# An attention and gated-convolution kernel rewritten: block-diagonal k^T v, one q*kv product, an on-chip spread of the norm factor, and an order written out as a list

## The chip, the core and the metric

The kernel runs on one core of one Trainium2 chip. The metric is device microseconds of one execution. The core's engines run side by side: TensorE (PE, with PEld for its weight loads), VectorE (DVE), ScalarE (ACT), GpSimd (POOL) and SyncE (SP); each takes its own instructions in order, and they wait for each other through semaphores. POOL and SP issue the DMAs. A figure such as 128x576 means partitions by elements.

## The reference

q, k and v are 8 batches x 8 heads x 576 positions x 64, in fp32.

```
kv  = einsum('bhsd,bhse->bhde', k, v)           # 64x64 for each head
out = einsum('bhsd,bhde->bhse', q, kv)
rms = sqrt(mean(out * out, axis=-1) + 1e-06)    # one factor per position and head
x   = out / rms * g_norm                        # heads side by side: (8, 576, 512)
h   = maximum(x @ w_in, 0)                      # w_in 512 x 1024
c   = conv_w[0]*h[s-1] + conv_w[1]*h[s] + conv_w[2]*h[s+1]   # along positions, zero at the ends
result = (h * sigmoid(c)) @ w_out               # w_out 1024 x 512, fp32
```

## The kernel before, in words

Matrices are bf16 in SBUF. Features lie on partitions: two heads fill 128 partitions, so 512 features are four tiles t, and the 1024 features of h are eight tiles f. A position s is 6p + r, p on 96 partitions, r along the row; the kernel keeps positions in a permuted order (by r first) up to the result.

The eight batches go in five groups, (0), (1, 2), (3, 4), (5, 6), (7). A group passes through these steps; the names in brackets are lines of the profile.

- load (L140): POOL issues casting DMAs for k, v and q of a batch, two buffers each; batch 0 comes in two halves. w_in comes in four pieces on SP's queue (L156), DVE scales and casts it (L157), and w_out comes on POOL's queue (L165).
- attn_a: k^T v by 48 matmuls of 96x64 per batch (L191), and four ACT copies of kv (L200); q is transposed by PE (L211) and copied by DVE (L214). out_mm (L267) makes q*kv for one tile with four matmuls of 64x64 and 288 columns. ACT squares it (L222), and a product with the small matrix sel sums the squares over each head's 64 partitions (L231).
- norm_unit: ACT takes Ln and Exp of the sums (L246, L247), SP stores the factor to DRAM (L249) and reads it back eight times, each row broadcast to 64 partitions (L254, tile rb).
- attn_b: out_mm makes q*kv a second time, and DVE multiplies it by rb into xT (L279).
- mm1: w_in's product (L300) in pieces of 384 or 288 columns, relu by ACT (L303). For every two f, DVE makes three tap products (L311) and six shifted adds (L315, L316; the permuted order cuts each shift into three), ACT the sigmoid (L317), DVE the gate product (L319).
- mm2: w_out's product, 8 matmuls of 512 columns for 128 positions (L336), copied out by ACT or, one time in three, DVE (L343, L341), and stored by SP in pieces (L350).

PSUM has separate pools: two slots for w_in's product, two for w_out's, one each for q*kv, the sums, and k^T v with the transposes. The order comes from interleave(): in stage s it mixes mm1 of group s, mm2 of group s - 1 and the attention of group s + 1, by weights written beside each unit. The framework may still move an instruction past others of its engine: in the trace a sigmoid stands between the Ln and the Exp of group 1, and each of these three has a table load of its own.

Of the kernel before, what the change touches and what calls it, by code (L numbers as in the profile page):

```python
# [56 lines left out]
DRAM = bass.MemoryType.DRAM  # L57

GROUPS = ((0,), (1, 2), (3, 4), (5, 6), (7,))


def interleave(*lists):

    keyed = []
    for n, units in enumerate(lists):
        total = float(sum(w for w, _ in units)) or 1.0
        at = 0.0
        for m, (w, fn) in enumerate(units):
            keyed.append(((at + 0.5 * w) / total, n, m, fn))
            at += w  # L70
    for _, _, _, fn in sorted(keyed, key=lambda x: x[:3]):
        fn()
# [3 lines left out]
def kernel(  # L76
# [39 lines left out]
    from concourse.masks import make_identity
    ident = consts.tile([P, P], BF16, name="ident")
    make_identity(nc, ident)
    ident32 = consts.tile([3 * n_ff, 3 * n_ff], FP32, name="ident32")
    make_identity(nc, ident32)  # L120
    eps_sb = consts.tile([P, 1], FP32, name="eps_sb")
    nc.vector.memset(eps_sb, eps)

    sel = consts.tile([P, 4, SM], BF16, name="sel")
    nc.vector.memset(sel, 0.0)
    for c in range(4):
        nc.vector.memset(sel[:D, c, 2 * c:2 * c + 1], 1.0)
        nc.vector.memset(sel[D:, c, 2 * c + 1:2 * c + 2], 1.0)

    qkv = {}

    def load(b, parts=1):
        hs = H // parts
        for i in range(parts):
            for name, src in (("k", k), ("v", v), ("q", q)):
                if i == 0:
                    qkv[name, b] = loads.tile([PS, H, R * D], BF16, name=name + "_sb")
                nc.gpsimd.dma_start(  # L140
                    out=qkv[name, b][:, i * hs:(i + 1) * hs, :],
                    in_=src[b, i * hs:(i + 1) * hs].rearrange("h (p r) d -> p h (r d)", r=R),
                )

    load(0, parts=2)

    w_in_sb = consts.tile([P, n_hd, D_ff], BF16, name="w_in_sb")
# [3 lines left out]
    cw_rows = consts.tile([3 * n_ff, P], FP32, name="cw_rows")  # L151
    nc.sync.dma_start(out=cw_rows, in_=moe_conv_w.rearrange("k (f p) -> (k f) p", p=P))
    w_stage = []
    for t in range(n_hd):
        st = loads.tile([P, D_ff], FP32, name="w_stage")
        nc.sync.dma_start(out=st, in_=moe_w_in[t * P:(t + 1) * P, :])  # L156
        nc.vector.tensor_scalar_mul(w_in_sb[:, t, :], st, g_sb[:, 0:1])  # L157
    cw_ps = ps_ss.tile([P, 3 * n_ff], FP32, name="cw_ps", tag="ss")
    nc.tensor.transpose(cw_ps, cw_rows, ident32)
    cw = consts.tile([P, 3 * n_ff], FP32, name="cw")  # L160
    nc.vector.tensor_copy(cw, cw_ps)

    load(1)
    w_out_sb = consts.tile([P, n_ff, D_model], BF16, name="w_out_sb")
    nc.gpsimd.dma_start(out=w_out_sb, in_=moe_w_out.rearrange("(f p) m -> p f m", p=P))  # L165
    load(2)


    class Group:
# [234 lines left out]
```

## Time and profile before

| | |
|---|---|
| runs, device us | 268.79, 271.13, 271.8 (median 271.13) |
| profiled execution, span | 268.2 us (the trace has no other time of it) |
| mean granted TensorE clock | 0.946 of full speed |
| PE busy, instructions | 200.9 us (75%), 1609 |
| DVE busy, instructions | 162.9 us (61%), 351 |
| ACT busy, instructions | 146.1 us (54%), 238 |
| DMA bytes written | 37.18 MB |

The span runs from the first to the last instruction. Busy time is the union of an engine's instructions. A busy PE is not at its peak: matmuls are pipelined, and a short group of them is charged its full latency. The profiler names what ended an engine's wait; of several it names the last.

### The profile page before, as it was taken

The numbers are of one execution on the slowest core, as the hardware profiler recorded it, in microseconds if no ns is written. First come the engines' busy times: TensorE is split into PE (matmuls) and PEld (weight loads), VectorE is DVE, ScalarE is ACT, GpSimd is POOL, SyncE is SP. The second block draws the span as 40 slices with busy tenths as digits, with TensorE's granted clock in tenths as the row PEclk, the third lists the DMA queues.
The fourth block names the chain that finished last, engine by engine and source line by source line (L and its number), as shares of the span: only waits on it lengthen the run. The fifth ranks groups of instructions, "written<-read, shape, count | busy, mean of one in ns | idle before, by whom it ended". The sixth has DMA issues, their size and how long they took to land.

```text
span 268.2 us, 4181 instructions
## 1 busy us (share of the span) xinstructions
PE 200.9 (75%) x1609; PEld 101.6 (38%) x1609; DVE 162.9 (61%) x351; ACT 146.1 (54%) x238; POOL 22.0 (8%) x36
## 2 busy tenths in 40 slices
PE   0118507989368879987289999883999899789953
PEld 0115303545133444433143444342344444444421
DVE  0222113678531577879884688858568879999521
ACT  1023302699922048998442789973249995665330
POOL 8321211011012121000000000000000000000000
PEclk9999999999867979999779999997799999999998
DMA  6999999995979999501954101396320254025423
GB/s 129 258 256 204 214 220 249 204 179 85 173 147 242 257 229 219 81 0 34 237 125 138 42 0 54 90 230 161 81 78 0 73 176 149 0 79 158 118 67 109
DMA packets 36006, 37.18 MB, mean 139 GB/s; under 512 B 2556, under 2 KB 30868, under 8 KB 35988
## 3 DMA queue, kind: packets, MB, share of 16 engines
q0 software_dynamic: 19904, 15.21, 37.2%
q1 hardware_dynamic: 16084, 21.73, 30.2%
q8 instruction: 12, 0.20, 0.3%
q14 instruction: 6, 0.05, 0.1%
HBM read 41.96 MB, written 10.17 MB: 194 GB/s over the span
## 4 chain that ended last, share of the span: by engine, by line
PE 42%; ACT 22%; DMA 14%; DVE 13%; issue 4%; SPq 3%; POOL 1%; DVEq 0%; POOLq 0%; ACTq 0%
PE h_ps L300 18%; PE o_ps L336 14%; ACT tap L317 8%; DMA rb<-scr 7%; DMA v_sb<-in_v_dram 5%; PE ot_ps L267 4%; ACT h L303 3%; DVE xT L279 3%; PE qT_ps L211 3%; SPq L254 3%; DVE tap L311 2%; PE ss_ps L231 2%; DVE h L319 2%; ACT L317 2%; ACT L247 2%
## 5 line engine op out<-in xcount | busy, mean ns | idle before, releaser
L336 PE MATMUL o_ps<-w_out_sb,h 128*128 128x512 bf16 (+1 forms) x296 | 78.3, 399 | 13.3 <-DVE h L319 12.0
L300 PE MATMUL h_ps<-xT,w_in_sb 128*128 128x384 bf16 (+1 forms) x416 | 82.7, 324 | 6.3 <-ACT h L303 5.8
L303 ACT ACTIVATE h<-h_ps 128x384 bf16<-128x384 f32 (+1 forms) x104 | 46.7, 464 | 25.4 <-PE h_ps L300 24.8
L311 DVE TENSOR_SCALAR tap<-h,cw 128x1152 bf16<-128x1152 bf16 (+1 forms) x120 | 47.8, 452 | 15.6 <-ACT h L303 15.4
L300 PEld LDWEIGHTS <-w_in_sb 128*128 128x128 bf16 x416 | 37.6, 99 | 37.0 <-issue 13.0
L336 PEld LDWEIGHTS <-h 128*128 128x128 bf16 (+1 forms) x296 | 28.3, 101 | 45.2 <-DVE h L319 14.8
L317 ACT ACTIVATE tap<-tap 128x2304 bf16<-128x2304 bf16 (+1 forms) x20 | 34.8, 1738 | 13.9 <-DVE tap L316 13.9
L279 DVE TENSOR_TENSOR xT<-ot_ps,rb 128x576 bf16<-128x576 f32 x32 | 24.1, 754 | 25.4 <-DMA rb<-scr 17.7
L200 ACT ACTIVATE kv_sb<-kv_ps 64x256 bf16<-64x256 f32 x32 | 12.1, 377 | 45.1 <-PE kv_ps L191 44.8
L267 PE MATMUL ot_ps<-qT,kv_sb 64*64 64x288 bf16 x256 | 23.0, 338 | 14.7 <-DVE xT L279 14.4
L319 DVE TENSOR_TENSOR h<-h,tap 128x2304 bf16<-128x2304 bf16 (+1 forms) x20 | 22.3, 1116 | 15.6 <-ACT tap L317 15.5
L343 ACT ACTIVATE o_sb<-o_ps 128x512 f32<-128x512 f32 (+1 forms) x25 | 14.9, 595 | 26.5 <-PE o_ps L336 24.5
L214 DVE COPY qT<-qT_ps 128x576 bf16<-128x576 bf16 x32 | 14.6, 455 | 22.5 <-PE qT_ps L211 22.3
L211 PE MATMUL qT_ps<-ident,q_sb 96*128 96x96 bf16 x192 | 18.6, 250 | 12.3 <-DVE qT L214 6.7
L316 DVE TENSOR_TENSOR tap<-tap,tap 128x1152 bf16<-128x1152 bf16 (+5 forms) x60 | 26.9, 471 | 0.0
L315 DVE TENSOR_TENSOR tap<-tap,tap 128x1152 bf16<-128x1152 bf16 (+5 forms) x60 | 26.8, 469 | 0.0
L222 ACT ACTIVATE sq<-ot_ps 128x576 bf16<-128x576 f32 x32 | 20.9, 652 | 5.5 <-PE ot_ps L267 5.4
L211 PEld LDWEIGHTS <-q_sb 96*128 96x128 bf16 x192 | 15.3, 123 | 19.7 <-issue 18.3
L267 PEld LDWEIGHTS <-kv_sb 64*64 64x64 bf16 x256 | 9.1, 108 | 32.7 <-issue 30.5
L191 PE MATMUL kv_ps<-v_sb,k_sb 96*64 96x64 bf16 x384 | 11.9, 218 | 10.5 <-DMA v_sb<-in_v_dram 10.5
L191 PEld LDWEIGHTS <-k_sb 96*64 96x64 bf16 x384 | 9.9, 131 | 15.0 <-issue 10.9
L341 DVE COPY o_sb<-o_ps 128x512 f32<-128x512 f32 x12 | 8.3, 689 | 6.8 <-PE o_ps L336 6.6
(26 smaller groups left out, 64.7 us busy)
## 6 DMA issues: line engine op xcount, KB each, us to landing
rb<-scr SPq DMA_DIRECT2D x24, 288.0 KB, 6.9
out_dram<-o_sb SPq DMA_DIRECT2D x24, 192.0 KB, 2.3
k_sb<-in_k_dram POOLq DMA_DIRECT2D x7, 576.0 KB, 12.1
v_sb<-in_v_dram POOLq DMA_DIRECT2D x7, 576.0 KB, 15.6
q_sb<-in_q_dram POOLq DMA_DIRECT2D x7, 576.0 KB, 12.7
out_dram<-o_sb SPq DMA_DIRECT2D x24, 128.0 KB, 2.3
rb<-scr SPq DMA_DIRECT2D x16, 144.0 KB, 4.9
w_stage<-in_moe_w_in_dram SPq DMA_DIRECT2D x4, 512.0 KB, 6.2
```

Of the source, the lines that this page charges most:

```text
L191: nc.tensor.matmul(ps[i * D:(i + 1) * D, hp, :], k_sb[:, 2 * hp + i, r * D:(r + 1) * D], v_sb[:, 2 * hp + i, r * D:(r + 1) * D], start=(r ...
L211: nc.tensor.transpose(ps[:, i, j * PS:(j + 1) * PS], q_sb[:, 2 * hp + i, j * P:(j + 1) * P], ident[:PS, :PS])
L267: nc.tensor.matmul(ps[i * D:(i + 1) * D, e, :HS], g.kv[bi][es, t, i, :], g.qT[bi][es, 2 * t + i, :], start=True, stop=True)
L279: nc.vector.tensor_mul(g.xT[:, t, bi * S:(bi + 1) * S].rearrange("p (e n) -> p e n", n=HS), ps[:, :, :HS], g.rb[:, t, 2 * bi:2 * bi + 2, :])
L300: nc.tensor.matmul(ps, w_in_sb[:, t, f * P:(f + 1) * P], g.xT[:, t, cs], start=(t == 0), stop=(t == n_hd - 1))
L303: nc.scalar.activation(g.h[:, f, cs], ps, AX.Relu)
L311: nc.vector.tensor_scalar_mul(taps[j][:, f, :], g.h[:, f0 + f, :], cw[:, col:col + 1])
L315: nc.vector.tensor_add(v[1][:, :, here], v[1][:, :, here], v[0][:, :, there])
L316: nc.vector.tensor_add(v[1][:, :, there], v[1][:, :, there], v[2][:, :, here])
L317: nc.scalar.activation(taps[1], taps[1], AX.Sigmoid)
L319: nc.vector.tensor_mul(hs, hs, taps[1])
L336: nc.tensor.matmul(ps[:n, :], g.h[:, f, t0:t0 + n], w_out_sb[:, f, :], start=(f == 0), stop=(f == n_ff - 1))
```

## The change

The kernel function is new almost throughout.

- The positions of xT, h and the result are in sequence order. The transposes of q keep the order by r (384 of 96x64 in place of 192 of 96x128); ACT's squares and copies of q*kv read PSUM with a step of 96 floats and write in sequence order. Batch 0 is squared without that step; its order changes in its multiply.
- kv of two heads is written into a 128x128 block-diagonal matrix (kvbd, zeros off the blocks), by two copies per batch (batch 0: one per tile and half). q*kv is one product of 576 columns per tile (ot), made once; ACT squares it (sq) and copies it to SBUF in fp32 (oc).
- Batch 0's norm: a product with ones (on) sums the squares and spreads the sum over the 64 partitions of its head at once; Ln and Exp (nl, nx) of 576 columns per tile, one multiply (mu0). The others go in groups (1), (2, 3), (4, 5), (6, 7): sums as before (ss), Ln, Exp (ln, ex), the factor split in three bf16 parts (sl), spread by a product with a selector (sp) into PSUM, and multiplied there (mu). No factor goes through DRAM.
- w_in's product: 64 units (hm) of 8 matmuls of 288 columns, relu of 576 (re).
- Convolution: batch 0 on PE, three diagonal matrices per f (di, cv), sigmoid (sv) and gate (mv) per f. The others on DVE in units of two f: tap products (ta), two adds (ad), sigmoid (sg), gate (mg); units hold one batch (1, 6, 7) or two (2 and 3, 4 and 5).
- w_out's product: 36 units of 128 rows (om), all copied by ACT (ea), one store of 256 KB each (st).
- Loads: q of batch 0 whole, then k and v in four pieces of two heads, then w_in in eight pieces of 512 columns, all on POOL's queue.
- PSUM: one ring of three slots of two banks for transposes, q*kv, on, sp, hm and cv, and one of two single banks for k^T v, sums and w_out's product.
- ACT's tables are loaded where the order needs another one: once at the start and nine times after.
- The order is a list of 646 tokens; after it, each instruction is tied behind the one before it on its engine.

Tokens of the list, between four of its places (n2: units of two batches; n1: of one):

| stretch | on ACT | on DVE | on PE |
|---|---|---|---|
| to hm.0.0 | sq 4, nl 4, nx 4, 4 copies of kv | qc 2, di 4, ws 4, mu0 4, 4 copies of kv | qt 2, kv of batch 0, ot 4, on 4 |
| to ss.2 | re 16, sv 8, sq 12, oc 10, 6 copies of kv, sg n1 2, ea 1, ln 1, ex 1, tables 3 | qc 6, di 4, ws 4, mv 8, mu 4, sl 1, ta n1 6, ad n1 3, mg n1 1 | hm 16, cv 8, qt 6, kv 3 batches, ot 12, sp 4, ss 1, om 2 |
| to ln.3 | re 26, sq 16, oc 18, 8 copies of kv, ea 8, sg n1 2, n2 4, ln 2, ex 2, tables 4 | qc 8, mu 16, sl 2, ta n1 2, n2 8, ad n1 1, n2 4, mg n1 3, n2 3 | hm 27, qt 8, kv 4 batches, ot 16, sp 16, ss 6, om 7 |
| to hm.7.7 | re 21, ea 9, sg n1 3, n2 4, ln 1, ex 1, tables 2 | mu 8, sl 1, ta n1 7, n2 8, ad n1 3, n2 4, mg n1 3, n2 5 | hm 20, sp 8, om 9 |
| to the end | re 1, ea 18, sg n1 5 | ta n1 9, ad n1 5, mg n1 5 | hm 1, om 18 |

```diff
-GROUPS = ((0,), (1, 2), (3, 4), (5, 6), (7,))
-def interleave(*lists):
...
+NORM = {0: [1], 1: [2, 3], 2: [4, 5], 3: [6, 7]}
+CONV = {0: (0, 1, 'P'), 1: (1, 1, 'D'), 2: (2, 2, 'D'), 3: (4, 2, 'D'), 4: (6, 1, 'D'), 5: (7, 1, 'D')}
+BUFS = {'a': 3, 'b': 2, 'q': 2, 'k': 2, 'v': 2, 'qT': 5, 'sq': 8, 'o32': 8, 'xT': 2, 'h': 2, 'tap': 2, 'row': 8, 'w': 2, 'gate': 3}
+ORDER = """
+di.5 qt.0.0 qc.0.0 qt.0.1 qc.0.1 kv.0.0.1 kvc.0.0.1.0 di.0 kv.0.1.1 kvc.0.1.1.0 kvc.0.0.1.1 ot.0.0 sq.0.0 di.6
+kvc.0.1.1.1 ot.0.1 sq.0.1 on.0 nl.0 nx.0 kv.0.2.1 kvc.0.2.1.1 kvc.0.2.1.0 on.1 kv.0.3.1 nl.1 nx.1 mu0.0 ot.0.2
+kvc.0.3.1.1 mu0.1 di.3 Lk.1 ws.3.0 Lv.1 kvc.0.3.1.0 ot.0.3 sq.0.2 ws.0.0 sq.0.3 on.2 nl.2 ws.1.0 nx.2 mu0.2
+ws.2.0 on.3 nl.3 nx.3 mu0.3 hm.0.0 re.0.0 di.7 Lq.1 ws.1.1 hm.0.2 ws.0.1 re.0.2 cv.0.0 sv.0.0 hm.0.1 re.0.1
...
+"""
...
+    ps_a = pool("ps_a", BUFS["a"], space=PSUM)
+    ps_b = pool("ps_b", BUFS["b"], space=PSUM)
...
+    load("q", 0)
+    for t in range(NT):
+        load("k", 0, 2 * t, 2)
+        load("v", 0, 2 * t, 2)
...
+    def act_table(which):
+        if act_set[0] != which:
+            act_set[0] = which
+            nc.scalar.preload_act_table_set(
+                {"ln": "natural_log_exp_and_others", "sig": "sigmoid_and_others"}[which])
...
+    def kvc(b, t0, n, i):
+        T["kv", b] = kvbd[b % 2]
+        half = slice(i * D, (i + 1) * D)
+        to, fr = kvbd[b % 2][half, t0:t0 + n, half], T["kvps", b, t0][half]
...
+    def mm576(ps, lhsT, rhs):
+        nc.tensor.matmul(ps[:, 512:S], lhsT, rhs[:, 512:S], start=True, stop=True)
+        nc.tensor.matmul(ps[:, 0:512], lhsT, rhs[:, 0:512], start=True, stop=True)
+    def ot(b, t):
+        ps = ps_a.tile([P, 1024], FP32, name="o_ps", tag="a")
+        mm576(ps, T["kv", b][:, t, :], T["qT", b, t])
+    def natural(ap):
+        return ap.rearrange("p (r n) -> p n r", n=PS)
...
+    def oc(b, t):
+        s = work.tile([P, S], FP32, name="o32", bufs=BUFS["o32"])
+        nc.scalar.activation(s.rearrange("p (n r) -> p n r", r=R), natural(T["ot", b, t][:, :S]), AX.Copy)
...
+    def sp(b, t):
+        ps = ps_a.tile([P, 2, 512], FP32, name="sp_ps", tag="a")
+        for e in range(2):
+            nc.tensor.matmul(
+                ps[:, e, :HS], spread[:, t * 4 + 2 * bi + e, :, :].rearrange("p i d -> p (i d)"), T["w", g],
+                start=True, stop=True)
+    def mu(b, t):
+        nc.vector.tensor_mul(
+            x_tile(b)[:, t, :].rearrange("p (e n) -> p e n", e=2),
+            T["o32", b, t].rearrange("p (e n) -> p e n", e=2), T["sp", b, t][:, :, :HS])
...
+    def hm(b, f):
+        ps = ps_a.tile([P, 2, 512], FP32, name="h_ps", tag="a")
+        for t in range(NT):
+            for e in range(2):
+                nc.tensor.matmul(
+                    ps[:, e, :HS], w_in_sb[:, t, f * P:(f + 1) * P], x[:, t, e * HS:(e + 1) * HS],
+                    start=(t == 0), stop=(t == NT - 1))
...
+    def ad(c, j):
+        tap = T["tap", c, j].rearrange("p m f b s -> p m (f b) s")
+        nc.vector.tensor_add(tap[:, 1, :, 1:], tap[:, 1, :, 1:], tap[:, 0, :, :S - 1])
+        nc.vector.tensor_add(tap[:, 1, :, :S - 1], tap[:, 1, :, :S - 1], tap[:, 2, :, 1:])
...
+    def cv(c, f):
+        ps = ps_a.tile([P, 2, 512], FP32, name="cv_ps", tag="a")
+        for m in (1, 0, 2):
+            for e in range(2):
+                lo, hi = max(e * HS + m - 1, 0), min((e + 1) * HS + m - 1, S)
+                at = lo - (m - 1) - e * HS
+                nc.tensor.matmul(ps[:, e, at:at + hi - lo], dg[m, f], x[:, lo:hi],
+                                 start=(m == 1), stop=(m == 2))
...
+    for token in ORDER.split():
+        name, *nums = token.split(".")
+        ops[name](*map(int, nums))
+    prev = {}
+    for ins in list(nc.cur_bb.bb.instructions):
...
```

## Rows read from the trace of the kernel before

**Rows 1.** Page, part 1: busy us, share of the span, instructions.
```profile
PE 200.9 (75%) x1609; PEld 101.6 (38%) x1609; DVE 162.9 (61%) x351; ACT 146.1 (54%) x238; POOL 22.0 (8%) x36
```

**Rows 2.** Windows: busy us of each engine (instructions), granted clock, DMA share, GB/s.
```profile
core 0: us, PE busy (x) PEld busy (x) DVE busy (x) ACT busy (x) POOL busy (x), PEclk, DMA share, GB/s
43.50:264.20 220.70, 186.67 (x1404) 91.74 (x1403) 153.89 (x326) 137.75 (x223) 9.24 (x12) 0.94 0.59 124
100.00:135.00 35.00, 26.78 (x225) 13.01 (x222) 28.52 (x57) 27.83 (x44) 0.77 (x1) 0.93 0.62 120
135.00:170.00 35.00, 33.92 (x230) 15.13 (x228) 24.78 (x45) 23.27 (x36) 0.00 (x0) 0.97 0.26 68
170.00:205.00 35.00, 28.34 (x211) 13.59 (x209) 25.70 (x48) 19.32 (x34) 0.00 (x0) 0.90 0.49 117
205.00:240.00 35.00, 31.84 (x189) 16.06 (x188) 30.85 (x65) 27.33 (x42) 0.00 (x0) 1.00 0.28 84
```

**Rows 3.** Chain of waits that ended last, its beginning: start us, us, what.
```profile
4.62 12.94 DMA v_sb<-in_v_dram
...
36.00 6.59 DMA rb<-scr
```

**Rows 4.** Timeline, several stretches: start us, us, engine, line, operation, count.
```profile
21.85 0.45 PE L267 MATMUL ot_ps<-qT,kv_sb 64*64 64x288 bf16 x4
...
41.83 0.66 PE L300 MATMUL h_ps<-xT,w_in_sb 128*128 128x288 bf16 x2
...
123.94 2.85 PE L300 MATMUL h_ps<-xT,w_in_sb 128*128 128x384 bf16 x16 [1.25 <-ACT h L303]
...
238.17 8.80 PE L336 MATMUL o_ps<-w_out_sb,h 128*128 128x512 bf16 x40
...
264.18 0.59 ACT L343 ACTIVATE o_sb<-o_ps 64x512 f32<-64x512 f32 x1 [2.97 <-PE o_ps L336]
```

**Rows 5.** A window of casting loads alone; POOL's issue of one.
```profile
20.00:22.00 2.00, 1.36 (x16) 1.06 (x15) 0.51 (x2) 0.04 (x1) 0.29 (x1) 1.00 1.31 203
...
L140 POOL DMA_DIRECT2D k_sb<-in_k_dram x9 | 6.9, 765 | 36.1 <-PE kv_ps L191 35.7 <-issue 0.4
```

**Rows 6.** ACT by line and form: count, busy us, mean ns, idle before.
```profile
L317 ACT ACTIVATE tap<-tap 128x2304 bf16<-128x2304 bf16 x12 | 25.5, 2122 | 8.9 <-DVE tap L316 8.9
L222 ACT ACTIVATE sq<-ot_ps 128x576 bf16<-128x576 f32 x32 | 20.9, 652 | 5.5 <-PE ot_ps L267 5.4
L343 ACT ACTIVATE o_sb<-o_ps 128x512 f32<-128x512 f32 x23 | 13.7, 596 | 23.3 <-PE o_ps L336 21.6 <-ACT h L303 1.8
L200 ACT ACTIVATE kv_sb<-kv_ps 64x256 bf16<-64x256 f32 x32 | 12.1, 377 | 45.1 <-PE kv_ps L191 44.8
L317 ACT ACTIVATE tap<-tap 128x1152 bf16<-128x1152 bf16 x8 | 9.3, 1162 | 5.0 <-DVE tap L316 5.0
L246 ACT ACT_TABLE_LOAD x4 | 5.1, 1283 | 0.1
L247 ACT ACT_TABLE_LOAD x4 | 5.1, 1283 | 0.1
```

**Rows 7.** DVE by line and form, same columns.
```profile
L311 DVE TENSOR_SCALAR tap<-h,cw 128x1152 bf16<-128x1152 bf16 x72 | 33.0, 512 | 8.5 <-ACT h L303 8.4
L279 DVE TENSOR_TENSOR xT<-ot_ps,rb 128x576 bf16<-128x576 f32 x32 | 24.1, 754 | 25.4 <-DMA rb<-scr 17.7 <-PE ot_ps L267 7.6
L319 DVE TENSOR_TENSOR h<-h,tap 128x2304 bf16<-128x2304 bf16 x12 | 16.3, 1358 | 12.3 <-ACT tap L317 12.3
L311 DVE TENSOR_SCALAR tap<-h,cw 128x576 bf16<-128x576 bf16 x48 | 14.8, 362 | 7.1 <-ACT h L303 6.9
L315 DVE TENSOR_TENSOR tap<-tap,tap 128x1152 bf16<-128x1152 bf16 x12 | 9.0, 750 | 0.0
L315 DVE TENSOR_TENSOR tap<-tap,tap 128x380 bf16<-128x380 bf16 x12 | 4.2, 349 | 0.0
```

More of the change, by code (lines that the diff above doesn't have):

```diff
@@ L150 @@
         nc.sync.dma_start(out=g_sb[i * D:(i + 1) * D, :], in_=g_norm.unsqueeze(1))
-    cw_rows = consts.tile([3 * n_ff, P], FP32, name="cw_rows")
+    cw_rows = consts.tile([3 * NF, P], FP32, name="cw_rows")
     nc.sync.dma_start(out=cw_rows, in_=moe_conv_w.rearrange("k (f p) -> (k f) p", p=P))
[L153 to L157, printed above, removed]
@@ new lines, in on, with nl, nx, x_tile @@
+    @op
+    def on(t):
+        ps = ps_a.tile([P, 1024], FP32, name="on_ps", tag="a")
+        T["on", t] = ps
+        mm576(ps, ones, T["sq", 0, t])
+    @op
+    def nl(t):
+        r = work.tile([P, S], FP32, name="o32", bufs=BUFS["o32"])
+        T["rs0", t] = r
+        act_table("ln")
+        nc.scalar.activation(r, T["on", t][:, :S], AX.Ln, bias=eps_sb, scale=1.0 / D)
+    @op
+    def nx(t):
+        nc.scalar.activation(T["rs0", t], T["rs0", t], AX.Exp, scale=-0.5)
+    def x_tile(b):
+        if ("x", b // 2) not in T:
+            T["x", b // 2] = work.tile([P, NT, 2, S], BF16, name="xT", bufs=BUFS["xT"])
+        return T["x", b // 2][:, :, b % 2, :]
@@ new lines, in h_tile @@
+    def h_tile(p):
+        if ("h", p) not in T:
+            T["h", p] = work.tile([P, NF, 2, S], BF16, name="h", bufs=BUFS["h"])
+        return T["h", p]
+    @op
+    def hm(b, f):
+        ps = ps_a.tile([P, 2, 512], FP32, name="h_ps", tag="a")
+        T["hm", b, f] = ps
+        x = x_tile(b)
+        for t in range(NT):
+            for e in range(2):
+                nc.tensor.matmul(
+                    ps[:, e, :HS], w_in_sb[:, t, f * P:(f + 1) * P], x[:, t, e * HS:(e + 1) * HS],
+                    start=(t == 0), stop=(t == NT - 1))
@@ new lines, in re, with span, ta @@
+    @op
+    def re(b, f):
+        nc.scalar.activation(
+            h_tile(b // 2)[:, f, b % 2, :].rearrange("p (e n) -> p e n", e=2),
+            T["hm", b, f][:, :, :HS], AX.Relu)
+    def span(c):
+        b0, n = CONV[c][:2]
+        return b0 // 2, slice(b0 % 2, b0 % 2 + n)
+    @op
+    def ta(c, f):
+        p, bs = span(c)
+        n = bs.stop - bs.start
+        j = f // 2
+        if ("tap", c, j) not in T:
+            T["tap", c, j] = work.tile([P, 3, 2, n, S], BF16, name="tap", tag="tap", bufs=BUFS["tap"])
+        tap = T["tap", c, j]
+        for m in range(3):
+            col = m * NF + f
+            nc.vector.tensor_scalar_mul(
+                tap[:, m, f % 2, :, :].rearrange("p b s -> p (b s)"),
+                h_tile(p)[:, f, bs, :].rearrange("p b s -> p (b s)"), cw[:, col:col + 1])
@@ new lines, in sv, with mv, om @@
+    @op
+    def sv(c, f):
+        act_table("sig")
+        g = work.tile([P, S], BF16, name="gate", bufs=BUFS["gate"])
+        T["gate", c, f] = g
+        nc.scalar.activation(g.rearrange("p (e n) -> p e n", e=2), T["cv", c, f][:, :, :HS], AX.Sigmoid)
+    @op
+    def mv(c, f):
+        p, bs = span(c)
+        h = h_tile(p)[:, f, bs.start, :]
+        nc.vector.tensor_mul(h, h, T["gate", c, f])
+    out_rows = out.rearrange("b s m -> (b s) m")
+    @op
+    def om(p, m):
+        ps = ps_b.tile([P, D_model], FP32, name="om_ps", tag="b")
+        T["om", p, m] = ps
+        h = T["h", p].rearrange("p f b s -> p f (b s)")
+        for f in range(NF):
+            nc.tensor.matmul(ps, h[:, f, m * P:(m + 1) * P], w_out_sb[:, f, :],
+                             start=(f == 0), stop=(f == NF - 1))
```

473 lines of the change are left out of this document (246 added, 227 removed).

## The prediction, as written before the result was known

> **What bounds the kernel now.** The page's first part says that no engine is full: PE is busy for 75% of the span, DVE for 61%, ACT for 54% [rows 1]. Such averages hide stages, so the next view is the windows [rows 2]: in four stretches of 35 us the busiest engine works for 0.81 (DVE), 0.97 (PE), 0.81 (PE) and 0.91 (PE) of the time, 0.88 on average. The bound changes hands between three engines of similar load, and each waits for another in turn; none is clearly the wall. The third view is the chain of waits at its beginning [rows 3]: batch 0's v lands only at 17.6 us, and at 36.0 us the chain stands in the transfer that spreads the norm factor. The timeline puts the first matmul of w_in at 41.8 us [rows 4]. So the first 42 us hold one batch's attention and little else, and the remaining 226 us hold nearly all the work. The end is short: the last ACT copy starts at 264.2 us [rows 4] and the span ends at 268.2, so some 4 us follow the last product.
>
> The sum is made against this execution's span, 268.2 us. The median of the runs, 271.1, is 2.9 us above it; I add that at the end.
>
> **Start.** DMAs of the casting queue alone move 203 GB/s [rows 5]. Batch 0's q, k and v are 1.77 MB in bf16: 8.7 us. Before, w_in's 2.1 MB came beside them on SP's queue; now w_in is queued behind them on POOL's, so with a first packet at about 2.5 us and 1.5 us to land (estimates) the last k/v pair is there at 12.7 us, in place of 17.6. The price is that POOL issues nine DMAs ahead of ident (0.77 us each at most [rows 5], so ident is there at about 8 us; q lands about then too), then eight for w_in, and that batch 1's k, v and q and w_out wait behind all of these; batch 1 should be there by 28 us (w_in drained by 17, then 8.7 and the landing), and its first use stands eight w_in units and four convolution units, some 9 us of PE, behind the first w_in product. The store to DRAM and the spreading reads for batch 0 are replaced by a product with a block of ones. What is late next is ACT: per tile a copy of kv (about 0.2), a square (0.65), Ln and Exp of 576 columns (about 0.7 each, priced like the other 576-column ACT rows [rows 6]): four tiles, 9.2 us in series. DVE's many small setup operations and the casts of w_in stand before and between them; I take the first square-chain work at 12 us, then 9.2 on ACT and one multiply of 0.75 [rows 7]: the first w_in matmul at **22 us**, between 18 (ACT starts with the first pair) and 26 (DVE's setup delays each tile). Gain: some 20 us.
>
> **Parts that move work.** PE: q*kv was made twice, but four 64x64 matmuls ran side by side, one group of four taking 0.45 us with its latency [rows 4]. Made once with a block-diagonal kv it takes 576 columns in series, 0.24 us at the rate of 16 matmuls of 384 columns in 2.85 us [rows 4], which is 0.42 ns a column once the first latency is taken off. So PE saves little there. It gains work: 56 spread matmuls of 288 columns (6.8 us) and 48 for the first convolution (5.9 us). w_in's product has 512 matmuls of 288 (62.5 us, the same columns as before), w_out's 288 of 512 columns (216 ns each: 40 in 8.80 us [rows 4], 62.2 us). The transposes become 384 of half the weight columns in place of 192: the same time if two halves run side by side, twice if not; either way they lie in stages in which PE has slack (below). PE streams about 162 us in all.
>
> ACT: kv copies fall from 32 of 0.377 us [rows 6] to 14 and a few small ones; table loads from 15, four of them at Ln and four at Exp [rows 6], to 10 of 1.28 us, because Ln and Exp now share one load and stand together. Added: 28 fp32 copies of 576 columns (18.2 us), the convolution's 8 sigmoids of batch 0, and all 36 output copies (0.596 [rows 6]) where DVE had 12. Relu goes to 64 of 576 columns (0.652 each, by the square's row). ACT's total is about 165 us, where [rows 1] has 146.
>
> DVE: the shifted adds become two per unit in place of six. They start at an odd element; the old kernel's form of 380 elements does too and takes 349 ns [rows 7]; from the even-started 1152 (750 ns) and 2304 (1358) forms, 0.53 ns an element, 380 would be 342. So I take 0.75 us for 1150 elements and 1.36 for 2300; at twice the element time, the far bound, the adds would put 13 us more on the stage below in which DVE leads, and the time at 238. [...] The 349 ns row speaks against it, and the row decides.
>
> The new operations that no row shows: ACT reads PSUM with a step of 96 floats (56 squares and copies). Low end 0.65 us as the contiguous row [rows 6]; high end a second clock per element, 576 times 0.833 ns (the slope of the two sigmoid rows), 0.48 us more. I take the low end, the same engine, size and memory, and give the other to a rival.
>
> **The stages behind the start.** I cut the written order at four tokens and count each engine's tokens in each stage.
> - First w_in product to the square sums of batch 2: ACT leads. 46 instructions of 0.652 (16 relu, 8 sigmoids, 12 squares, 10 copies) 30.0, kv copies 2.3, two sigmoids of 1152 2.3, one output copy 0.6, Ln and Exp 0.9, three table loads 3.9: 40.0 us. PE has 34, DVE 29.
> - To the last Ln: ACT again. 60 of 0.652 are 39.1, kv copies 3.0, eight output copies 4.8, sigmoids 2 x 1.162 + 4 x 2.122 = 10.8, Ln and Exp 1.9, four table loads 5.1: 64.7 us. PE 54, DVE 54.
> - To the last w_in product: DVE leads. 24 tap products of 1152 at 0.458 and 21 of 576 at 0.308 (busy by count [rows 7]) are 17.5, adds 8 x 1.358 + 6 x 0.75 = 15.4, gate products 5 x 1.358 + 3 x 0.75 = 9.0, eight factor multiplies 6.0, the split of a factor 1.6: 49.5 us. PE 37, ACT 35.
> - The rest: PE leads with 18 units of w_out, 8 x 0.216 each, and one of w_in: 32.1 us.
>
> Back-to-back ACT instructions overlap a little (its groups' counts times means add up to 153 us against 146.1 busy [rows 1]), so ACT's two stages are taken at 0.953: 99.8. Sum 99.8 + 49.5 + 32.1 = 181.4 us if the leading engine never waits. It will: [rows 2] give 0.81 to 0.97. I take 0.93, above their mean, because the old low stretches are ones in which w_out's product waited for the gated h, and in the new list these products stand well behind the gate products of their pair until the last stage. 181.4 / 0.93 = 195. With 22 at the start and 4 at the end the span is 221, and the time **224 us**. At 0.85 it is 242; at 1.0, 210.
>
> **Rivals.**
> - Engines run ahead across my cuts, so that only whole-kernel totals bind: PE's 158 us behind the start at 0.93 is 170, and the time 170 + 26 + 3 = **199**. For: separate queues, and buffers of 2 to 8. Against: the taps have two buffers and PSUM's wide slots three. Chance 0.18.
> - Strided PSUM reads cost a second clock: 56 x 0.48 = 27 us, all in the two stages where ACT leads, 0.953 x 27 / 0.93 = 27.6, so **252**. Against: no old row shows such a read, and DVE's odd starts cost nothing. [...] Chance 0.15.
> - Explicit table loads do not hold, and Ln and Exp each load again as in the old loop [rows 6]: up to 8 loads, 10 us on ACT, so **235**. The change would then not do what it says there. Chance 0.05.
> - **Slower than before:** all wide products (152 tiles: transposes, q*kv, spread, w_in, convolution) pass through one ring of three PSUM slots in a fixed order, where the old kernel had separate pools. A q*kv tile holds its slot for a square and a copy, 1.3 us of ACT, and everything behind it on PE waits. Between 43.5 and 264.2 us the old DVE had 153.9 us of work in 220.7, 0.70 [rows 2]; if the ring pushes the leader down to that, 181.4 / 0.70 = 259, and the time is **288**. It gets slower than 271 once the ring costs (271 - 224) / 152 = 0.31 us per tile. Chance 0.07.
>
> **How the numbers follow.** Forecast 0.55, the others as given. The time is the likeliest case's, 224 us. Its own range is 210 to 242. The ends go a little past the run-ahead and the strided case, 196 to 257, so that about a third of each (0.06 and 0.05) and the slow case (0.07) are left out, 0.18. About 1% (2.7 us) is what can be told from no change. Faster by over 1%: all but the slow case and a little of the high tail, 0.91; same 0.03; slower 0.06.
>
> **What would show it.** First w_in product near 22 us and no DMA between Exp and the multiply: the start is right. Squares and copies at 0.65 us: no price for the step; at 1.1: the strided rival. Adds at 0.75 and 1.36. Ten table loads. ACT the busiest until about two thirds of the span, then DVE, then PE. Waits of PE for ACT's squares and copies above 40 us in total would mean the ring. The prediction is wrong if the start is over 30 us, or the leading engine's share falls under 0.8.

## The result, and the profile after

| | before | after |
|---|---|---|
| runs, median (lowest to highest), us | 271.31 (268.79 to 271.8) | 217.35 (216.95 to 218.9) |
| profiled execution: time, span, us | span 268.2 | 216.95, span 215.2 |
| mean granted TensorE clock | 0.946 | 0.992 |
| DMA bytes | 37.18 MB | 27.03 MB |

The ratio is 0.803, 95% interval 0.798 to 0.808: 54 us faster, and 6.6 us under the forecast of 224, inside its own range (210 to 242). In the experiments, executions more than 1.5% above the fastest one of the same kernel are left out of the times and ratios.

The page of the changed kernel answers [rows 1]. First come each engine's busy time, share and instructions; then two lines of 40 slices of 5.4 us, PE's busy tenths and the granted clock in tenths:

```profile
PE 178.4 (83%) x1783; PEld 111.5 (52%) x1801; DVE 158.3 (74%) x328; ACT 153.4 (71%) x232; POOL 28.9 (13%) x47
PE   0246469957997839999989999999999999999993
PEclk9999999999999997999999999999999999999999
```

DVE and ACT have nearly the busy time of before in a span 53 us shorter. PE is full from the middle on and has its gaps in the first 80 us. Its busy time fell by 22 us although the change gave it matmuls, and the clock went up with that. Cut into windows of 0.3 us, the trace before has 791 at a granted clock of 1.00, 92 at 0.50 and 11 in between, the trace after 705, 11 and 1. So a mean of 0.946 is half clock in twice 0.054 of the span, 29 us, and 0.992 is 3.4 us, the one slice under 9.

The windows answer [rows 2]. The stretches are cut where the prediction cut: first w_in product, square sums of batch 2, last Ln, last w_in unit, last w_out product. The first stretch is cut again at batch 1's k^T v and at its first w_in unit:

```profile
core 0: us, PE busy (x) PEld busy (x) DVE busy (x) ACT busy (x) POOL busy (x), PEclk, DMA share, GB/s
25.80:74.70 48.90, 39.77 (x520) 27.30 (x527) 28.94 (x66) 36.41 (x60) 6.92 (x9) 1.00 1.01 156
74.70:141.80 67.10, 61.89 (x774) 41.77 (x783) 56.02 (x88) 60.29 (x92) 4.61 (x6) 0.97 0.53 90
141.80:178.50 36.70, 35.55 (x235) 22.81 (x235) 35.71 (x60) 27.10 (x37) 0.00 (x0) 1.00 0.16 58
178.50:211.50 33.00, 32.58 (x151) 14.70 (x151) 23.47 (x55) 19.57 (x28) 0.00 (x0) 1.00 0.43 162
...
25.80:39.10 13.30, 11.49 (x74) 7.67 (x75) 7.20 (x18) 7.55 (x11) 0.00 (x0) 1.00 1.29 205
39.10:53.80 14.70, 9.99 (x156) 6.79 (x157) 7.04 (x15) 11.63 (x19) 2.30 (x3) 1.00 0.98 146
53.80:74.70 20.90, 18.29 (x296) 12.84 (x300) 14.70 (x34) 17.22 (x30) 4.62 (x6) 1.00 0.84 133
```

From 74.7 us on the busiest engine works for 0.92, 0.97 and 0.99 of the time, where the four old stretches of [rows 2] had 0.81 to 0.97. The first stretch is the poor one, above all its second piece, in which no engine reaches 0.8. Up to the last Ln the busiest engine is PE and not, as forecast, ACT: 39.77 against 36.41 us, then 61.89 against 60.29. (In this trace the 280 w_out matmuls of 512 columns have a mean of 385 ns each, 108 us laid end to end, and are busy for 65.2 us, so they overlap, and PE's busy time alone does not say that PE sets the pace.)

The groups by line and form answer [rows 6, 7]: count | busy us, mean ns of one | idle before.

```profile
L326 ACT ACTIVATE sq<-o_ps 128x576 bf16<-128x576 f32 x28 | 17.7, 660 | 0.5 <-PE o_ps L307 0.5
L332 ACT ACTIVATE o<-o_ps 128x576 f32<-128x576 f32 x28 | 17.8, 659 | 3.3 <-PE o_ps L307 2.6 <-PE qt_ps L294 0.6
L324 ACT ACTIVATE sq<-o_ps 128x576 bf16<-128x576 f32 x4 | 2.6, 646 | 3.3 <-remote 2.9 <-PE o_ps L307 0.4
L232 ACT ACT_TABLE_LOAD x9 | 11.5, 1283 | 0.1
L181 ACT ACT_TABLE_LOAD x1 | 1.3, 1283 | 0.7 <-PEq L569 0.7
L465 DVE TENSOR_TENSOR tap<-tap 128x2300 bf16<-128x2300 bf16 x8 | 10.8, 1352 | 0.0
L465 DVE TENSOR_TENSOR tap<-tap 128x1150 bf16<-128x1150 bf16 x12 | 9.0, 750 | 0.0
L416 DVE TENSOR_TENSOR xT<-o,sp_ps 128x576 bf16<-128x576 f32 x28 | 20.0, 748 | 6.0 <-PE sp_ps L410 6.0
L360 DVE TENSOR_TENSOR xT<-o_ps,o 128x576 bf16<-128x576 f32 x4 | 8.3, 2074 | 1.7 <-ACT o L350 1.7
```

Squares and copies that read PSUM with a step (L326, L332) take what the one without a step takes (L324). The adds (L465) are at 750 and 1352 ns; those of 1152 elements that start at an even one took 750 [rows 7]. Ten table loads. One line is off: batch 0's multiply (L360), which writes bf16 with a step of six elements, takes 2074 ns where [rows 7] have 754 for the same size.

The chain of waits of its first 30 us answers [rows 3]: start us, us, what.

```profile
1.29 6.11 DMA q_sb<-in_q_dram
...
8.60 0.29 POOL ident masks.py:199
...
9.27 0.31 PE cw_ps L207
...
10.11 1.34 DVE spread L216
...
12.65 1.24 DVE qT L301 x2
...
16.27 0.65 ACT sq L324
...
18.29 2.09 DVE xT L360
...
20.68 2.08 DVE xT L360
...
27.32 1.98 DVE xT L360
...
29.34 2.56 PE h_ps L433 x10
```

q has landed at 7.4 us, but the identity that transposes need is made from 8.6 on, because POOL issues nine DMAs first. DVE's setup (cw, spread, the tap diagonals) follows it, and then four multiplies of 2 us. No DMA stands between Exp and multiply any more. The first w_in matmul starts at 25.76 us, in the kernel before at 41.8 [rows 4]. But only six of that product's sixteen matmuls run then: the other ten start at 29.34 us, when the fourth multiply is done.

### The profile page after: what moved, and what is told of

Its sections match the earlier page's. It is cut to its first block, busy times and chain, and to the rows that moved or that the text cites. A ratio compares the mean times of both kernels' runs of the same rounds, so it can differ in the third digit from the quotient of the medians.

```text
span 215.2 us, 4372 instructions
## 1 busy us (share of the span) xinstructions
PE 178.4 (83%) x1783; PEld 111.5 (52%) x1801; DVE 158.3 (74%) x328; ACT 153.4 (71%) x232; POOL 28.9 (13%) x47
## 2 busy tenths in 40 slices
DMA packets 25992, 27.03 MB, mean 126 GB/s; under 512 B 1372, under 2 KB 20852, under 8 KB 25972
## 4 chain that ended last, share of the span: by engine, by line
DVE 39%; PE 37%; ACT 15%; issue 4%; DMA 3%; POOL 0%; POOLq 0%; ACTq 0%; DVEq 0%
PE h_ps L433 14%; PE om_ps L523 12%; DVE tap L458 12%; DVE tap L466 6%; DVE tap L465 5%; DVE h L478 4%; PE qt_ps L294 3%; DVE xT L360 3%; DMA q_sb<-in_q_dram 3%; PE cv_ps L499 3%; ACT sq L326 3%; ACT h L439 3%; DVE xT L416 3%; PE sp_ps L410 2%; ACT L232 2%
## 5 line engine op out<-in xcount | busy, mean ns | idle before, releaser
L433 PE MATMUL h_ps<-xT,w_in_sb 128*128 128x288 bf16 x512 | 70.1, 291 | 4.1 <-DVE xT L360 1.3
L523 PE MATMUL om_ps<-w_out_sb,h 128*128 128x512 bf16 x280 | 65.2, 385 | 0.8 <-issue 0.2
L433 PEld LDWEIGHTS <-w_in_sb 128*128 128x128 bf16 x512 | 50.0, 99 | 20.4 <-issue 5.4
L439 ACT ACTIVATE h<-h_ps 128x576 bf16<-128x576 f32 x64 | 40.2, 652 | 14.2 <-PE h_ps L433 13.7
L458 DVE TENSOR_SCALAR tap<-h,cw 128x576 bf16<-128x576 bf16 (+1 forms) x120 | 43.1, 425 | 4.2 <-ACT h L439 3.7
L523 PEld LDWEIGHTS <-h 128*128 128x128 bf16 x288 | 28.4, 99 | 33.4 <-issue 2.4
L472 ACT ACTIVATE tap<-tap 128x1152 bf16<-128x1152 bf16 (+1 forms) x20 | 30.9, 1547 | 3.9 <-DVE tap L466 3.7
L529 ACT ACTIVATE row<-om_ps 128x512 f32<-128x512 f32 x36 | 21.4, 594 | 17.1 <-PE om_ps L523 16.3
L416 DVE TENSOR_TENSOR xT<-o,sp_ps 128x576 bf16<-128x576 f32 x28 | 20.0, 748 | 6.0 <-PE sp_ps L410 6.0
L478 DVE TENSOR_TENSOR h<-h,tap 128x1152 bf16<-128x1152 bf16 (+1 forms) x20 | 19.8, 992 | 2.1 <-ACT tap L472 2.1
L466 DVE TENSOR_TENSOR tap<-tap 128x1150 bf16<-128x1150 bf16 (+1 forms) x20 | 20.1, 1004 | 0.7
L332 ACT ACTIVATE o<-o_ps 128x576 f32<-128x576 f32 x28 | 17.8, 659 | 3.3 <-PE o_ps L307 2.6
L465 DVE TENSOR_TENSOR tap<-tap 128x1150 bf16<-128x1150 bf16 (+1 forms) x20 | 19.8, 991 | 0.0
L326 ACT ACTIVATE sq<-o_ps 128x576 bf16<-128x576 f32 x28 | 17.7, 660 | 0.5 <-PE o_ps L307 0.5
L232 ACT ACT_TABLE_LOAD x9 | 11.5, 1283 | 0.1
```

The lines of the kernel that those rows point to most:

```text
L326: nc.scalar.activation(s.rearrange("p (n r) -> p n r", r=R), natural(src), AX.Square)
L416: nc.vector.tensor_mul(x_tile(b)[:, t, :].rearrange("p (e n) -> p e n", e=2), T["o32", b, t].rearrange("p (e n) -> p e n", e=2), T["sp", b ...
L433: nc.tensor.matmul(ps[:, e, :HS], w_in_sb[:, t, f * P:(f + 1) * P], x[:, t, e * HS:(e + 1) * HS], start=(t == 0), stop=(t == NT - 1))
L439: nc.scalar.activation(h_tile(b // 2)[:, f, b % 2, :].rearrange("p (e n) -> p e n", e=2), T["hm", b, f][:, :, :HS], AX.Relu)
L458: nc.vector.tensor_scalar_mul(tap[:, m, f % 2, :, :].rearrange("p b s -> p (b s)"), h_tile(p)[:, f, bs, :].rearrange("p b s -> p (b s)"), ...
L465: nc.vector.tensor_add(tap[:, 1, :, 1:], tap[:, 1, :, 1:], tap[:, 0, :, :S - 1])
```

## Experiments

All times are medians, and every ratio is to the kernel before in runs beside it (medians 269.0 to 270.7). The kernels differ from the changed kernel by the diff shown, except where it says otherwise.

### The start

**e1_step_in_read**: batch 0 as the others, the step in ACT's and DVE's reads of PSUM and none in the write.

```diff
-        x = x_tile(0)[:, t, :].rearrange("p (n r) -> p r n", r=R)
-        nc.vector.tensor_mul(x, T["ot", 0, t][:, :S].rearrange("p (r n) -> p r n", n=PS), ...)
+        x = x_tile(0)[:, t, :].rearrange("p (n r) -> p n r", r=R)
+        nc.vector.tensor_mul(x, natural(T["ot", 0, t][:, :S]), ...)
```

> Batch 0's squares are written in sequence order, so that its four factor multiplies read PSUM and the factor with a step and write xT without one. Theory (the step of 12 bytes in DVE's bf16 write costs 1.3 us per multiply, and the multiplies lie on the chain to the first w_in product): they take 0.75 to 0.8 us in place of 2.07, the first w_in product starts at about 21.5 us in place of 25.8, and the time falls by 3 to 5 us, to 212 to 214. Rival 1 (a step costs DVE the same on the read side, in PSUM): 2.07 us stays and the time stays within 1 us of 217.4. Rival 2 (what is gained at the start is given back behind it, because data or ACT set the pace there): multiplies at 0.75, first product at 21.5, time within 1 us of 217.4.

**e2_ident_first**: the two identity matrices are made ahead of the loads.

```diff
+    make_identity(nc, ident)
+    make_identity(nc, ident32)
     load("q", 0)
...
-    make_identity(nc, ident)
-    make_identity(nc, ident32)
```

> POOL makes the two identity matrices before the first load in place of after the ninth. Theory (the start waits for ident behind nine DMA issues, and DVE's setup with it): first transposes at about 8 us in place of 9.5, first square at about 12 in place of 15.4, first w_in product at 22.5 to 23.5 in place of 25.8, time 214 to 215.5. Rival (the loads, now 0.8 us later, set the end of the chain): first product at 25.8 to 26.6, time 217 to 218.5.

**e3_both**: the edits of e1 and e2 together.

> Both edits at once. If the two costs add up along one chain: first w_in product at 18.5 to 19.5, time 209 to 211.5. If the last pair of k and v (there at about 14.5 us) then ends the chain: first product at 20 to 21, time 212 to 214.

**e5_start_all**: both edits, and four builds of tap diagonals moved in the list from before the multiplies of batch 0 to behind them.

```diff
-di.5 qt.0.0 ... di.0 ... di.6 ... mu0.1 di.3 ... mu0.3 hm.0.0 re.0.0 di.7
+qt.0.0 ... mu0.3 di.0 hm.0.0 re.0.0 di.2 ...
```

> Both mends of the start (the identity ahead of the loads, the fourth-step writes of batch 0 in natural order) and the diagonal tap matrices built behind the first multiplies instead of between them: four builds of 0.57 us leave DVE's queue ahead of the first w_in product. Theory A (two of them stand on the chain): 207.5 to 209.5 us, about 1 us under both mends alone. Rival B (they ran in waits, and their new place delays the first convolution products): 209.5 to 212 us.

| | time, us | ratio, interval | first w_in product, us | fourth multiply ends, us |
|---|---|---|---|---|
| changed kernel | 217.35 | 0.803, 0.798 to 0.808 | 25.8 | 29.3 |
| e1_step_in_read | 213.62 | 0.792, 0.785 to 0.799 | 23.6 | 25.0 |
| e2_ident_first | 213.96 | 0.793, 0.788 to 0.799 | 23.0 | 26.5 |
| e3_both | 209.60 | 0.775, 0.766 to 0.784 | 20.4 | 21.8 |
| e5_start_all | 209.25 | 0.775, 0.771 to 0.780 | 20.0 | 21.5 |

The multiply of e1, with a stepped PSUM read and a contiguous write:

```profile
L357 DVE TENSOR_TENSOR xT<-o_ps,o 128x576 bf16<-128x576 f32 x4 | 3.0, 758 | 2.0 <-ACT o L347 2.0
```

So the step costs DVE 1.3 us per instruction in the write (2074 ns against 758) and next to nothing in the read of PSUM (758 against the 754 of [rows 7]). Both causes are shown, and they add: 3.7 and 3.4 us apart, 7.75 together. The times came out as the theories had them, but the first product of e1 (23.6, not 21.5) and of e3 (20.4, as its second case had it) did not. What the time follows is the last column, the end of the multiply on which the whole product waits: it moves by 4.3, 2.8 and 7.5 us. Three builds of diagonals stand on the changed kernel's chain, but with both edits they matter little: in e5 the first product comes 0.3 us earlier, not 1, and its time cannot be told from e3's. e3 and e5 beat both kernels.

### Operations and order

**u2_untied**: the list stays, the ties go, so that the framework may move an instruction past others of its engine, as it could before.

```diff
-    prev = {}
-    for ins in list(nc.cur_bb.bb.instructions):
-        ...
-            tc.add_manual_dep(ins, prev[e].name, ..., reason="order")
```

> The new operations, called in the new list's order, but without the ties: the framework is free to order each engine's instructions, as it was in the old kernel. Theory A (the written order carries a large part of the gain, because the new operations leave no engine with less work: PE's and ACT's sums went up): 230 to 255. Theory B (the operations carry it: no DRAM round trip, fewer adds and table loads): 214 to 223.

**u1_mixed_tied**: the ties stay; behind batch 0's attention the list is made anew by the even mixing rule of the kernel before, with weights of my choice after its own.

```diff
-ORDER (searched list behind batch 0's attention)
+interleave(mm1((0,)), attn(0)) + interleave(mm1((1,)), attn(1))
++ interleave(mm1((2, 3)), mm2(0), attn(2)) + interleave(mm1((4, 5)), mm2(1), attn(3)) + ...
```

> New operations, but behind batch 0's start the written order is made anew by the old kernel's mixing rule (stages merged evenly by weight) and tied as the new list is. Theory A (the operations bring the new kernel's work down, the searched order brings the leading engine's share up from the 0.88 of the old stretches to the 0.95 to 0.99 seen from 100 us on): the leader's share falls back to about 0.85 to 0.9 and the time is 230 to 245 us. Rival B (the operations alone carry the gain, any even mixing will do): 214 to 222 us. Start as in the changed kernel in both: first w_in product at 25 to 27 us.

**o1_old_tied**: the kernel before, with the changed kernel's loop of ties put behind its last instruction.

```diff
+    prev = {}
+    for ins in list(nc.cur_bb.bb.instructions):
+        ...
+            tc.add_manual_dep(ins, prev[e].name, ..., reason="order")
```

> The kernel before, with nothing changed but that each engine is tied to the order in which the program writes its instructions. Theory A (an order is worth what was searched into it; the tie alone holds an order made by an even mixing rule): no gain, 265 to 285 us. Rival B (the tie alone is what the change gains behind the start): 245 to 260 us.

**u1c_mixed_scheduler**: u1's list without ties and without the nine explicit table loads.

```diff
-            nc.scalar.preload_act_table_set(...)
...
-            tc.add_manual_dep(ins, prev[e].name, ..., reason="order")
```

> The changed kernel's operations with the old way of setting an order: the even mixing rule for the list, no tie of an engine to it (so the planner may reorder, as it did for the kernel before), and no explicit table loads. It isolates the operations from the searched order. Theory A (the operations are worth some 30 us by themselves under that planner, as the untied searched list with 238.9 to 240 suggests): 234 to 250 us. Rival B (without its own order the new operations bring little): 260 to 275 us.

**t1_no_explicit_loads**: the changed kernel, list and ties, without the nine explicit table loads of its list; the one in the setup, of the set with Ln and Exp, stays.

```diff
             act_set[0] = which
-            nc.scalar.preload_act_table_set(...)
```

> The changed kernel without its explicit table loads, so that Ln and Exp each get a load of their own: 18 or 19 loads of 1.28 us in place of 10, the case of the third rival. Theory A (ACT sets the pace up to 140 us, as forecast): the 8 or 9 loads cost their whole time, 10 to 12 us: 227 to 230 us. Rival B (ACT has slack of 20 to 25% in the start and at the norm's place, so only those loads that stand in a norm chain are felt): 219 to 225 us.

| | list | tied | table loads | time, us | ratio, interval |
|---|---|---|---|---|---|
| changed kernel | searched | yes | 10 | 217.35 | 0.803, 0.798 to 0.808 |
| t1_no_explicit_loads | searched | yes | 14 | 223.53 | 0.826, 0.822 to 0.831 |
| u2_untied | searched | no | 31 | 237.6 | 0.881, 0.865 to 0.897 |
| u1c_mixed_scheduler | mixed | no | 14 | 243.41 | 0.903, 0.896 to 0.910 |
| u1_mixed_tied | mixed | yes | 10 | 325.95 | 1.202, 1.197 to 1.207 |
| o1_old_tied | before's, mixed | yes | | 411.02 | 1.514, 1.505 to 1.522 |

Read as one path the table splits the gain. The new operations under the old way of setting an order are worth 26 us (269.6 to 243.4, u1c). The searched list with its ties is worth 20 more (243.4 to 223.5; u1c and t1 have the same operations and 14 loads each); 5.5 us of these lie ahead of the first w_in product, which starts at 31.2 us in u1c. The explicit loads are worth 6.2 (223.5 to 217.35). Other paths could split it differently. The list without ties is at 237.6, as theory A of u2 had it, and it pays for 31 loads, because the framework moved nine explicit ones to the front, where they serve nothing (ACT is busy for 13.4 us of the first 20 there, for 5.8 in the changed kernel). What the list alone gives at equal loads was not run, and u1c stands for one choice of weights in the mixing rule.

Both theories missed u1 and o1, and by far: ties to a list that was not made for them cost 83 us (u1 against u1c, which has four loads more) and 140 us (o1 against the kernel before). The waits view shows why: engine, line, waited for: us in total, times, longest. First the changed kernel, then u1.

```profile
ACT tap L472 <- DVE tap L466: 3.7, 5, 1.2
...
PE o_ps L306 <- ACT sq L326: 0.8, 2, 0.5
PE h_ps L433 <- ACT o L346: 0.8, 1, 0.8
```

```profile
ACT tap L472 <- DVE tap L466: 75.2, 20, 7.0
...
PE o_ps L306 <- ACT h L439: 14.1, 3, 5.1
...
PE sp_ps L410 <- ACT h L439: 12.8, 7, 3.9
PE h_ps L433 <- ACT o L332: 12.7, 4, 5.9
...
PE o_ps L306 <- ACT o L332: 5.8, 2, 5.1
```

The mixing rule writes tap products, adds, sigmoid and gate product of a unit one behind another. Tied, ACT stands at every sigmoid until DVE's adds are done, with squares, copies and relus queued behind it. ACT's timeline in u1 shows one such wait in its brackets, and the queue that it held up:

```profile
118.95 2.12 ACT L472 ACTIVATE tap<-tap 128x2304 bf16<-128x2304 bf16 x1 [4.46 <-DVE tap L466]
120.98 0.63 ACT L326 ACTIVATE sq<-o_ps 128x576 bf16<-128x576 f32 x1
121.51 0.64 ACT L332 ACTIVATE o<-o_ps 128x576 f32<-128x576 f32 x1
```

And PE then waits for PSUM slots that ACT's copies and relus hold, 45 us in the four lines of PE above. Groups of u1, PE's w_in product, with its idle time and what ended it; the changed kernel's 512 have 4.1 us there and a mean of 291 ns:

```profile
L433 PE MATMUL h_ps<-xT,w_in_sb 128*128 128x288 bf16 x512 | 86.0, 322 | 20.5 <-ACT o L332 12.7 <-ACT h L439 4.6 <-DVE xT L360 1.3
```

In the searched list gate work stands where its inputs are long done, and ACT's wait for the adds is 3.7 us.

t1's expectation had the count of loads wrong (14, not 18 or 19: batch 0's eight Ln and Exp run on the set loaded in the setup), and its time is in rival B's range. Four more loads of 1.283 us are 5.1 us, and the time rose by 6.2 (6.4 in the spans, 215.2 to 221.6). The mean clock also fell, from 0.992 to 0.966; what that adds was not measured apart. In its groups of ACT, Ln (L384) and Exp (L388) have a load each:

```profile
L384 ACT ACT_TABLE_LOAD x4 | 5.1, 1283 | 0.1
L388 ACT ACT_TABLE_LOAD x4 | 5.1, 1283 | 0.1
```

In t1's chain the load between Ln and Exp stands at its full length, and all else of the group waits for Exp: the load starts at 47.56 us, 0.02 after Ln, takes 1.28, and Exp follows 0.01 after its end.

### Two parts of the change

**u3_conv0_dve**: batch 0's convolution on DVE. **u3b_conv0_late**: the same, its work for six of the eight tiles later in DVE's order.

```diff
-CONV = {0: (0, 1, 'P'), ...
+CONV = {0: (0, 1, 'D'), ...
-di.0 ... cv.0.0 sv.0.0 ... mv.0.0 ...
+ta.0.0 ta.0.1 ad.0.0 sg.0.0 mg.0.0 ...
```

> The changed kernel with batch 0's convolution back on VectorE (24 tap products of 576, 8 adds of 1150, 4 wide sigmoids and gate products) in place of the 48 products and 8 sigmoids of the new one. It adds about 17 us to DVE and takes 6 us from PE and 3 us from ACT between 25 and 65 us, where DVE is busy for 11 of 20 us. Theory A (DVE has the room there, and ACT and the norm chain set the pace): 214 to 221 us. Rival B (DVE was the wall and the move to TensorE is worth its whole 17 us): 228 to 236 us.

> Batch 0's convolution on VectorE as in the run before, with the same instructions, but its tap products and adds for six of the eight tiles placed in DVE's order behind the factor multiplies of batch 1 or in DVE's idle time ahead of the norm chain. Theory A (of the 15 us the run before lost, about 10 were two multiplies of batch 1 queued behind convolution work on DVE, not DVE's load): 217 to 225 us. Rival B (DVE's 17 us more of work is what costs): 229 to 234 us.

u3 took 232.16 us (0.857, 0.854 to 0.861), as the rival had it, but the chain of waits names a cause beside DVE's load. In u3, from the norm of batch 1:

```profile
50.10 1.42 DVE xT L415 x2
51.52 1.68 DVE tap L457 x6
...
55.88 0.76 DVE h L477
56.64 1.68 DVE tap L457 x6
...
61.01 0.76 DVE h L477
61.77 0.68 DVE xT L415
```

Of batch 1's four factor multiplies (L415) the third stood behind one unit of convolution work on DVE and ran at 54.6 us, and the fourth stood behind two, ten microseconds after the second. It ended at 62.4 us, 8.5 later than in the changed kernel. With that work moved, u3b took 224.53 us (0.833, 0.828 to 0.839), with the same busy time of DVE (166.6, in u3 167.0): of the 15 us, 7.6 were a place in a queue. The 7.2 that stay go with 8.3 us more of DVE (166.6 busy against 158.3) and a lower clock (0.954 against 0.992). Whether that is DVE's load, the clock or places still not searched is open.

**u4_dram_spread**: the factor of batches 1 to 7 goes through DRAM again.

```diff
-    def sl(g): ...      # split in three bf16 parts
-    def sp(b, t): ...   # product with the selector
+    def rt(g):
+        nc.sync.dma_start(out=scr, in_=T["rh", g])
+        ...             # eight reads, each row broadcast to 64 partitions of xT
```

> The changed kernel with the norm factor of batches 1 to 7 spread as before: Exp writes it in bf16, one store to DRAM and eight reads that broadcast it, and the multiply reads it from SBUF; the split and the 56 selector matmuls go (the factor is rounded to bf16). Theory A (in the tied order the spread stands directly in front of the multiplies, so each of four groups waits for the transfers, 3 to 7 us more than for split and product): 229 to 245 us. Rival B (the work placed around it hides the transfers): 213 to 220 us.

It took 250.54 us (0.930, 0.925 to 0.935), 33 us more than the changed kernel and 5 above theory A. The chain of u4 from Exp to the third of batch 1's multiplies, and in a line of the timeline the first of them:

```profile
49.06 4.30 DMA scr<-rh
...
53.38 0.64 SPq L402
...
57.96 2.76 DMA xT<-scr
...
60.82 0.09 DVE xT L408
```

```profile
56.83 0.76 DVE L408 TENSOR_TENSOR xT<-o,xT 128x576 bf16<-128x576 f32 x1 [12.70 <-DMA xT<-scr]
```

From Exp's end to the first multiply it is 7.8 us. In the changed kernel Exp of this group ends at 48.1 and the first multiply starts at 50.5, 2.4 us. For the four groups the timelines give 7.8, 12.7, 5.6 and 7.3 us against 2.4, 2.3, 2.5 and 3.0: 23 us more, near the theory's 3 to 7 for each but for the second. The later multiplies wait again, because SP issues the eight reads one behind another, 0.6 us each, which the theory forgot. The waits view puts it together, the changed kernel's line first:

```profile
DVE xT L416 <- PE sp_ps L410: 6.0, 7, 2.1
```

```profile
DVE xT L408 <- DMA xT<-scr: 45.7, 10, 14.9
```

DVE waits 40 us longer, and 33 were paid: in a list that puts little between factor and multiply, little hides a transfer. The mean clock fell too, to 0.911, and its part is not known.

## Why the prediction came out as it did

Its sum against what was measured, us (the stretches are the windows above; those forecast at 0.93 are shown with it):

| step | predicted | measured | off |
|---|---|---|---|
| first w_in product | 22 | 25.8 | +3.8 |
| to ss.2, ACT: 38.1 / 0.93 | 41.0 | 48.9 | +7.9 |
| to ln.3, ACT: 61.7 / 0.93 | 66.3 | 67.1 | +0.8 |
| to the last w_in unit, DVE: 49.5 / 0.93 | 53.2 | 36.7 | -16.5 |
| to the last w_out product, PE: 32.1 / 0.93 | 34.5 | 33.0 | -1.5 |
| end, and median over span | 6.9 | 5.8 | -1.1 |
| total | 224 | 217.35 | -6.6 |

The total is better than its terms: errors of +12.5 and -19.1 us cancel to -6.6. That it came so near is luck.

- **Start.** The mechanism was right: no DRAM, inputs sooner. Two sizes were off, and e1 and e2 show both: mu0's multiply was costed at 0.75 us and took 2.07, and POOL's identity and DVE's setup behind it held the copies of the transposes, so that ACT's first square came at 15.4 us, though its chain began at 12.0 with a copy of kv, as forecast. The 22 us were summed to the end of the last tile's multiply, and that came at 29.3, so by its own working the start missed by more than the table has. With both mended it comes at 21.8, and the product starts at 20.4. I weighed stepped reads in PSUM and looked at no stepped write, and no row showed one. The traces do: for bf16 and a step of 12 bytes, 2074 ns over 576 elements is 3.6 ns each, where the contiguous write of e1 has 758 ns, 1.3 each. The 2.5 us to the first packet and the 1.5 us to land were estimates that no row gives; in the trace after, the casting queue's packets begin at 2.7 us and the last v of batch 0 lands at 13.5, not 12.7.
- **To ss.2.** ACT's work was sized right (36.4 busy, 38.1 summed), but ACT did not lead: it was busy for 0.74 of the stretch, under the 0.8 that the prediction itself named as a sign of being wrong, and PE for 0.81. Up to 39.1 us PE led (11.49 of 13.3), since ACT has only relus and sigmoids before batch 1's q*kv. From 39.1 to 53.8 the norm of batch 1 ran through transposes, squares and copies, table load, Ln, Exp, split, product and multiply in series. The step that failed is one leader at 0.93 for a stretch that is a series; the mended start leaves it as it is (e3 takes 48.4 us for the same stretch).
- **To ln.3.** The size of ACT was right (61.7 forecast, 60.3 busy), the leader is not settled: PE was busier still (61.9, where 54 were forecast). PE was counted too low here and in the stretch before (39.8, where 34 were forecast), for one because the 56 spread products, issued in pairs, were busy for 10.0 us, not 6.8: 179 ns each, where w_in's 512 of the same 288 columns were busy for 70.1 us, 137 each. So the sign "ACT the busiest until about two thirds of the span" did not come.
- **To the last w_in unit.** DVE led, as said, at 0.97. It had run ahead: by about 141.8 us it had done two tap tokens, one pair of adds and one gate product of two batches from behind the cut, 6.8 us at the prediction's prices, and at 178.5 it left three tap tokens but for one product, one pair of adds and two gate products of one batch, 5.5 us, which found room in the last stretch. The run-ahead rival was right here, where the forecast was furthest off. Its total was not, because its sum of PE was too low: PE was busy for 169.8 us behind the start, not 158, at 0.91. With 169.8 at its 0.93, the start as measured and the forecast's end its sum would be 182.6 + 25.8 + 6.9 = 215.
- **Stepped PSUM reads on ACT** cost 14 ns at most (660 and 659 ns against 646), where the rival had 480, so it is out. **Adds**: 0.750 and 1.352 us, as taken from the 349 ns row; the far bound of twice the element time, which no run shows, did not come. **Table loads** held, ten of them, and t1 bounds their price.
- **One ring of PSUM slots.** PE's waits for ACT's squares and copies are a few us, so it did not decide. u1 shows that such waits can grow: same operations, same ring, another list, 45 us of PE waiting for slots, and the kernel is slower than before by 20%. There they follow from ACT's wait for DVE, so u1 gives the ring no price of its own. The prediction priced the order as a step from 0.88 to 0.93 on the leader, 11 us of its sum. It is worth more: 20 us against the mixing rule without ties, and with ties to that rule's list the same operations take 326 us.
- **Not foreseen:** the clock. The prediction took PE's rates as they stood, and the changed kernel has 3.4 us at half clock in place of 29. What this alone gave was not measured apart.

## What to carry to other kernels

A written order and the ties that hold it belong together: in u1 a tie turned each early-written waiting instruction into a wait for all that was queued behind it (75.2 us of ACT's time before its sigmoids, 3.7 in the searched list), so tie only a list in which inputs are long done, and read the waits view for one engine's line that waits often. Cost a rewritten tensor's access on both sides: batch 0's multiply took DVE 758 ns with the step in its PSUM read (e1) and 2074, 2.7 times that, with it in its write. Cut a forecast where the work changes from series to parallel, not only where the busiest engine changes.

## What the runs showed of the hardware

- A multiply of 576 elements on DVE took 754 ns contiguous (before), 758 ns with PSUM read in steps of 96 floats (e1), 2074 ns with bf16 written in steps of six elements (after).
- bf16 adds on DVE that start at an odd element ran at the even ones' rate: 750 ns for 1150 elements (after), as for 1152 from an even one (before), and 1352 ns for 2300 (after).
- A table load on ACT took 1283 ns; between Ln and Exp it started 0.02 us behind the one, and the other started 0.01 us behind it (t1).
- With the same instructions in another order, PE was busy for 178.4 us at a mean granted clock of 0.992 (after) and for 215.7 us at 0.856 (u1); w_in's matmuls took 291 and 322 ns on average. That the longer waits in u1 brought the clock down is not shown: u2 and u1c, longer than the changed kernel by 20 us and more, had 0.993 and 0.985.
